# Turning the last eight row blocks of LN(x) with transposing DMAs instead of TensorE

## The chip, the cores and the metric

The kernel runs on one core of a Trainium2 chip. The time is that of the whole launch on the device in microseconds (us); a lower one is better. A core has five engines that each work through a queue of their own in order: TensorE (PE, matmuls), VectorE (DVE), ScalarE (ACT), GpSimd (POOL) and SyncE (SP), which here issues nearly all DMAs. They wait for each other by semaphores.

## The reference

The block computes, for 2048 tokens of width 512:

```python
h  = x + A(layernorm(x))            # A: 32 heads of 16, full softmax, then wo
h2 = h + B(layernorm(h))            # B: a gated MLP (gMLP) with a 2048x2048 mixing over tokens
# A:
qkv = (LN(x) @ wqkv)                # x: [2048, 512], wqkv: [512, 1536]
p = softmax(q @ k.T * 16**-0.5);  o = p @ v;  out = o @ wo
# B:
z = gelu(LN(h) @ w_in);  z1, z2 = halves of z
g = w_sp @ layernorm(z2) + b_sp;  out = (z1 * g) @ w_out
```

All inputs and the output are float32. The change concerns the first step alone: `LN(x)` and its way into the products with `wqkv`.

## The kernel before

**Precision.** A float32 matrix is held as two float16 matrices, a high part (the value rounded) and a low part (what the rounding left). A product is three matmuls (`mm3`, L107 to L109): high by high, high by low, low by high.

**The prologue** makes `LN(x)`, turns it so that the features lie on the partitions (`xT`, high part `xT[0]`, low part `xT[1]`), and multiplies it with `wqkv`. The 2048 rows are 16 blocks of 128 (block `sb`). For one block:

- `load_x` fetches it (tile `xg`), `stats` (L385, DVE) takes its mean and variance, `scales` computes the reciprocal root for four blocks at once (about a dozen tiny DVE instructions, L114 to L131, and `nb`, L401).
- `normal` (L412, ACT) normalizes the block in place.
- `turn_x` is `turn_only` (four 128x128 float32 transposes on PE, L424, into the PSUM tile `tp`) and `put_x`: ACT copies `tp` to the high part (L433), and DVE subtracts that from `tp` into the low part (L431).

A projection is 12 matmuls over 512 columns into one PSUM bank `acc`, of which there are three in turn. `proj_v(sb)` makes the rows of v of one block; `take_v` (DVE, L492) copies them out and SP stores them (L493, `v_scr`). `proj_qk(b, n, i)` makes k (i = 1) or q (i = 0) of a quarter n (blocks 4n to 4n+3) for the weight column block b; its take is a high part on ACT (L458), a low part on DVE (L461), and a store on SP (L464). For k with n < 2, `sums` makes two more ACT copies (`kf`, L472 and L473), later a sum on GpSimd (L476 to L479). The take of a projection is written into the middle of the next one.

**The weights** of the q and k columns come by column block b: `load_wqk(b)` (SP, L345, two DMAs of 256 KB), `weigh_wqk(b)` (two DVE reductions, L352, then two GpSimd products `each`, L356), `measure(b)` (a PE matmul, L374, then small DVE instructions), and `put_wqk(b)`, which scales and splits them. Block 0 is used in the loop below; block 1 is loaded in its last round.

**Order.** Every engine's order is the order of the code (`manual_schedule`); nothing is sorted later. The loop around the change runs over `g` = 0, 1, 2 with a = 4g and b = 4g+4, so that round g multiplies blocks a to a+3 and prepares blocks b to b+3. Below, v8 is `proj_v(8)`, and k2 and q2 are the products of quarter 2. PE's order in the rounds is: round 1: v4 to v7, k1, q1; round 2: v8 to v11, k2, q2; then v12, `measure(1)`, v13, k3, q3, v14, v15. After that come 24 projections for b = 1 to 3, among which the first row maxima of the attention are taken, and the attention itself from about 160 us.

In each round 1 and 2 the blocks b, b+1 are normalized before k and q, and turned inside q; blocks b+2, b+3 are normalized after q and turned inside the first v projection of the next round (or of the code after the loop).

Of the kernel before, what the change touches and what calls it, by code (L numbers as in the profile page):

```python
# [11 lines left out]
F16 = mybir.dt.float16  # L12
I32 = mybir.dt.int32
AF = mybir.ActivationFunctionType
# [5 lines left out]
P = 128  # L20
S = 2048
D = 512
# [8 lines left out]
DB = D // P  # L31
# [28 lines left out]
def block_kernel(ctx: ExitStack, tc: tile.TileContext, x, wqkv, wo, w_in, w_sp4, b_sp, w_out, out):  # L60
# [7 lines left out]
    nc = tc.nc  # L68
# [118 lines left out]
    def load_q(g):  # L187
        hg, qb = divmod(g, NQ)
        c = slice(qb * 512, (qb + 1) * 512)
        qst[g] = qpool.tile([RG + KM, 2, 512], F16, name="qst")  # L190
        for j in range(3):
            for t in range(2):
                h0 = DH * head(hg, 0, t)
                nc.sync.dma_start(
                    qst[g][RG * t + j:RG * t + KS:3, :, :],
                    q_scr[(0, 1, 0)[j], h0:h0 + 2 * DH, c].rearrange("(p r) s -> r p s", r=DH))
# [72 lines left out]
    with ExitStack() as pre:  # L269
        p2 = pre.enter_context(tc.tile_pool(name="pre_2", bufs=2))  # L270
        pc = pre.enter_context(tc.tile_pool(name="pre_c", bufs=1))
# [2 lines left out]
        pt = pre.enter_context(tc.tile_pool(name="pre_pt", bufs=2, space=PSUM))  # L274
        more[3] = more[4] = lambda: pt.tile([P, 512], F32, name="tp")

        xT = [pc.tile([P, DB, S], F16, name=f"xT{i}") for i in range(2)]
        wv = [pc.tile([P, DB, D], F16, name=f"wv{i}") for i in range(2)]
        w4 = wqkv.rearrange("(a p) c -> p a c", p=P)
        xs, xns, wqk, wvs = {}, {}, {}, {}  # L280
# [3 lines left out]
        def load_x(sb):  # L284
            xs[sb] = p2.tile([P, D], F32, name="xg", tag="row", bufs=10)
            nc.sync.dma_start(xs[sb], x[sb * P:(sb + 1) * P, :])
# [53 lines left out]
        def load_wqk(b):  # L340
            raws[b] = []
            for i in range(2):
                t = p2.tile([P, 512], F32, name="wg", tag="row", bufs=10)
                t = t.rearrange("p (a c) -> p a c", a=DB)
                nc.sync.dma_start(t, w4[:, :, i * D + b * P:i * D + (b + 1) * P])  # L345
                raws[b].append(t)

        def weigh_wqk(b):

            most = p2.tile([P, 2], F32, name="most")  # L350
            for i in (1, 0):
                nc.vector.tensor_reduce(most[:, i:i + 1], raws[b][i], axis=AX.XY, op=ALU.max,  # L352
                                        apply_absolute_value=True)
            each = p2.tile([P, 2, P], F32, name="each")
            for i in range(2):
                nc.gpsimd.tensor_scalar(each[:, i], ident, most[:, i:i + 1], 1.0,  # L356
                                        op0=ALU.mult, op1=ALU.mult)
            measures.append(lambda: measure(b, each))

        def put_wqk(b):  # L360

            wqk[b] = [p2.tile([P, 2, DB, P], F16, name=f"wqk{i}") for i in range(2)]
            for i in (1, 0):
                hi, lo, t, by = wqk[b][0][:, i], wqk[b][1][:, i], raws[b][i], sizes[b][:, i:i + 1]
                if b:
                    nc.gpsimd.tensor_scalar(t, t, by, 1.0, op0=ALU.mult, op1=ALU.mult)
                    split(hi, lo, t, "pool", "pool")
                else:
                    scaled(hi, lo, t, by, None if i else "pool")
# [11 lines left out]
        def stats(mv, *blocks):  # L381

            for sb in blocks:
                st = p2.tile([P, 6], F32, name="st")
                nc.vector.bn_stats(st, xs[sb])  # L385
                nc.vector.bn_aggr(mv[0][:, len(mv) - 1, :], st)
                mv.append(sb)

        def moments(n):
            return [p2.tile([P, n, 2], F32, name=f"mv{n}")]  # L390

        def scales(mv, between=lambda: None):

            t, *blocks = mv
            n = len(blocks)
            rs = rstd_of(p2, t[:, :, 1], n, between, up=HN_UP)
            nb = p2.tile([P, n], F32, name=f"nb{n}")
            if n == 1:
                nc.vector.tensor_scalar(nb, rs, t[:, 0, 0:1], -1.0, op0=ALU.mult, op1=ALU.mult)
            else:  # L400
                nc.vector.scalar_tensor_tensor(nb, t[:, :, 0], -1.0, rs, op0=ALU.mult, op1=ALU.mult)  # L401

            def normal(*which, on="act"):

                for sb in which:
                    j = blocks.index(sb)
                    xns[sb] = xs.pop(sb)
                    if on == "dve":
                        nc.vector.tensor_scalar(xns[sb], xns[sb], t[:, j, 0:1], rs[:, j:j + 1],
                                                op0=ALU.subtract, op1=ALU.mult)  # L410
                        continue
                    nc.scalar.activation(xns[sb], xns[sb], AF.Identity,  # L412
                                         bias=nb[:, j:j + 1], scale=rs[:, j:j + 1])

            return normal
# [3 lines left out]
        def turn_only(sb):  # L419

            xn = xns.pop(sb)
            tps[sb] = tp = pt.tile([P, 512], F32, name="tp").rearrange("p (d s) -> p d s", d=DB)
            for d in range(DB):
                nc.tensor.transpose(tp[:, d, :], xn[:, d * P:(d + 1) * P], ident)  # L424

        def put_x(sb, *which):

            c = slice(sb * P, (sb + 1) * P)
            for i in which:
                if i:  # L430
                    nc.vector.tensor_sub(xT[1][:, :, c], tps[sb], xT[0][:, :, c])  # L431
                else:
                    nc.scalar.activation(xT[0][:, :, c], tps[sb], AF.Copy)  # L433

        def turn_x(*blocks):

            for sb in blocks:
                turn_only(sb)
                put_x(sb, 0, 1)
# [108 lines left out]
        def proj(kind, *which, then=lambda: None, at=1, **kw):  # L548

            def between(d):  # L550
                if d == 0 and rest:
                    rest.pop(0)()
                if d == 1:
                    if takes:
                        takes.pop(0)()
                if d == at:
                    then()

            takes.append(kind(*which, between, **kw))
# [11 lines left out]
        normal = scales(mv[0])  # L571
        normal(0, on="dve")
        measure_wv()
        turn_only(0)
        stay_warm(3)
        put_x(0, 0)
        normal(1, on="dve")
        put_wv(0, "act")
# [4 lines left out]
        stay_warm(2)  # L583
        put_wv(1, "act")
        put_x(0, 1)
        put_x(1, 0)
        normal(2, 3)
# [24 lines left out]
        for g in range(3):  # L612
            a, b = 4 * g, 4 * g + 4
            mv = moments(4)
            if g:
                proj(proj_v, a)
                turn_x(a + 2, a + 3)
                if g == 1:
                    load_x(14)
                    load_x(15)  # L620
                stats(mv, b, b + 1)
                proj(proj_v, a + 1)
                stats(mv, b + 2, b + 3)
                proj(proj_v, a + 2)
                normal = scales(mv)
                normal(b, b + 1)
                proj(proj_v, a + 3)
            else:
                proj(proj_v, 2, on_act=True)
                stats(mv, 4, 5, 6)  # L630
                measures.pop(0)()
                stats(mv, 7)
                put_wqk(0)
                proj(proj_v, 3, on_act=True)
            if g == 1:
                load_q(0)
            proj(proj_qk, 0, g, 1)
            if not g:
                normal = scales(mv)
                normal(b, on="dve")  # L640
                normal(b + 1)
            if g == 2:
                load_wqk(1)
            proj(proj_qk, 0, g, 0, then=lambda: turn_x(b, b + 1), at=1 if g else 2)
            if not g:
                load_x(12)
                load_x(13)
            normal(b + 2, b + 3)
        weigh_wqk(1)
        proj(proj_v, 12)  # L650
        turn_x(14, 15)
        load_wqk(2)
        load_wqk(3)
        measures.pop(0)()
# [12 lines left out]
        for j in range(24):  # L667
            b, n, i = 1 + j // 8, j // 2 % 4, 1 - j % 2
# [119 lines left out]
    with ExitStack() as at:  # L788
# [256 lines left out]
        for n in range(0, len(units), 2):  # L1045
# [53 lines left out]
            for tok in PAIR if len(later) < 2 else ():  # L1099
                i = int(tok[-1]) if tok[-1].isdigit() else 0  # L1100
# [16 lines left out]
                elif tok == "H":  # L1117
                    a = 0 if first else 256
# [47 lines left out]
    with ExitStack() as mid:  # L1166
# [73 lines left out]
        with tc.manual_schedule(engines={E.PE, E.Activation, E.DVE, E.Pool, E.SP}):  # L1240
# [3 lines left out]
            for k in range(NB):  # L1244
                sb, new = row[k], row.get(k + 2)
# [358 lines left out]
```

## Time and profile before

| | |
|---|---|
| runs | 1713.07, 1714.01, 1714.47 us; median 1714.01 |
| profiled execution, first to last instruction (span) | 1712.3 us |
| PE busy | 1699.5 us, 99% |
| DVE / ACT / POOL busy | 85% / 77% / 48% |
| granted TensorE clock | full throughout |

The span is the time from the first to the last instruction of the one execution that was profiled, and the trace gives no other time for it; the median of the runs is 1.7 us above it. Times in rows count from the span's start. A row of the timeline reads: start, length, engine, line and operation, output<-inputs, sizes, how many instructions are merged in it (x2), and in brackets how long the engine stood idle before it and what released it. SPq is SP's issue of DMAs; its length is that of the issuing, not of the transfer.

### The profile page before, as it was taken

What the parts mean: (1) busy time and instruction counts of PE and PEld (TensorE: products, weight loads), DVE (VectorE), ACT (ScalarE), POOL (GpSimd) and SP (SyncE); (2) the same over time, 40 slices, a digit from 0 to 9 for tenths busy, and PEclk for the clock granted to TensorE, in tenths of its full rate; (3) what the DMA queues carried; (4) which work ended last, traced back from release to release, by engine and by line L of the source; (5) the groups of instructions that cost most, each with busy time, mean ns of one, the idle gap of its engine ahead of it and who ended that gap; (6) DMA issues with size and microseconds to landing.
All of it is one profiled execution on the core that took longest, in us unless ns stands there. A gap on an engine that the chain in (4) does not pass through costs nothing.

```text
span 1712.3 us, 36689 instructions
## 1 busy us (share of the span) xinstructions
PE 1699.5 (99%) x13508; PEld 644.7 (38%) x13508; DVE 1452.5 (85%) x3051; ACT 1317.5 (77%) x2584; POOL 813.6 (48%) x1062
## 2 busy tenths in 40 slices
PE   9999999999999999999999999999999999999999
PEld 4533222222222222222222222222225666656665
DVE  7688999999999999999999999999936787543444
ACT  4334999999999999999999999999995545211111
POOL 1231867776673267687767776400002766300100
PEclk9999999999999999999999999999999999999999
DMA  5534332342221244344434444300114454664551
GB/s 185 167 94 144 103 89 68 101 94 82 81 68 25 56 118 117 104 144 125 130 113 124 132 140 130 80 13 19 37 39 124 140 173 140 233 234 156 198 217 44
DMA packets 189309, 196.03 MB, mean 114 GB/s; under 512 B 67496, under 2 KB 140008, under 8 KB 189128
## 3 DMA queue, kind: packets, MB, share of 16 engines
q1 hardware_dynamic: 186824, 188.04, 36.8%
q10 hardware_dynamic: 2304, 5.64, 0.8%
q8 instruction: 106, 1.74, 0.4%
q14 instruction: 75, 0.61, 0.1%
HBM read 122.10 MB, written 65.93 MB: 110 GB/s over the span
## 4 chain that ended last, share of the span: by engine, by line
PE 78%; DVE 12%; DMA 3%; POOL 2%; ACT 2%; SPq 2%; issue 1%; ACTq 0%; POOLq 0%; DVEq 0%
PE pv L830 26%; PE s L805 17%; PE m L223 9%; DVE mx L228 7%; PE acc L107 4%; PE g L108 4%; PE g L109 4%; PE g L107 4%; PE acc L109 4%; PE acc L108 4%; DMA rc<-r_scr 1%; DVE ab L237 1%; DVE og L840 1%; SPq L723 1%; DVE rs_t L124 1%
## 5 line engine op out<-in xcount | busy, mean ns | idle before, releaser
L814 ACT ACTIVATE pt<-s 128x512 f32<-128x512 f32 x1968 | 1006.2, 637 | 5.5 <-PE m L223 4.3
L228 DVE TENSOR_REDUCE mx<-m 128x1 f32<-128x512 f32 x1510 | 947.5, 682 | 11.7 <-PE m L223 2.9
L805 PE MATMUL s<-qst,kst 50*128 50x512 f16 x2048 | 604.2, 379 | 0.2
L830 PE MATMUL pv<-pt,vst 128*32 128x256 f32 (+1 forms) x6056 | 598.1, 466 | 4.1 <-DVE og L840 1.3
L223 PE MATMUL m<-kst,qst 48*128 48x512 f16 x1510 | 452.4, 381 | 0.0
L805 PEld LDWEIGHTS <-kst 50*128 50x128 f16 x2048 | 132.0, 94 | 352.1 <-issue 323.7
L830 PEld LDWEIGHTS pv<-pt,vst 128*32 128x32 f32 x6056 | 119.5, 108 | 290.7 <-issue 277.3
L223 PEld LDWEIGHTS <-qst 48*128 48x128 f16 x2048 | 159.2, 93 | 173.6 <-issue 124.2
L223 PE MATMUL m<-uvs,qst 48*128 48x512 f16 x504 | 190.5, 380 | 0.6 <-DVE mx L228 0.6
L245 POOL TENSOR_SCALAR nm<-nm 128x16 f32<-128x16 f32 x32 | 6.6, 206 | 358.8 <-DVE nm L242 358.8
L237 DVE CUSTOM_DVE_ANT_0 ab<-m,ab 128x512 f32<-128x512 f32 x252 | 170.5, 677 | 2.7 <-ACT ab L233 2.7
L233 ACT ACTIVATE ab<-m 128x512 f32<-128x512 f32 x252 | 157.3, 624 | 15.5 <-PE m L223 14.8
L1368 ACT ACTIVATE pr<-pr,up 128x304 f32<-128x304 f32 (+1 forms) x32 | 17.0, 574 | 109.2 <-DVE up L1322 109.2
L991 POOL TENSOR_TENSOR op<-raw,op 128x512 f16<-128x512 f32 x80 | 92.9, 1161 | 6.0
L914 POOL TENSOR_TENSOR raw<-raw 128x512 f32<-128x512 f32 (+1 forms) x84 | 83.3, 991 | 6.7
L919 POOL TENSOR_TENSOR acc_sp<-acc_sp,raw 128x512 f32<-128x512 f32 x63 | 80.4, 1277 | 4.5
L109 PE MATMUL acc<-wi,hT 128*128 128x344 f16 x256 | 79.1, 309 | 0.3 <-DVE hT L104 0.3
L107 PE MATMUL acc<-wi,hT 128*128 128x344 f16 x256 | 79.1, 309 | 0.0
L108 PE MATMUL acc<-wi,hT 128*128 128x344 f16 x256 | 79.1, 309 | 0.0
L1510 POOL TENSOR_TENSOR pr<-pr,z 128x344 f32<-128x344 f32 x8 | 7.3, 914 | 145.9 <-DMA whole<-squares 108.3
L911 POOL TENSOR_SCALAR raw<-raw 128x512 f32<-128x512 f32 (+1 forms) x88 | 52.3, 594 | 19.7 <-DMA raw<-in_wqkv 12.4
L1509 DVE TENSOR_TENSOR pr<-g,v 128x344 f32<-128x344 f32 x8 | 4.1, 517 | 66.6 <-PE g L109 63.5
(247 smaller groups left out, 2292.9 us busy)
## 6 DMA issues: line engine op xcount, KB each, us to landing
raw<-in_w_sp SPq DMA_DIRECT2D x128, 256.0 KB
s_scr<-op SPq DMA_DIRECT2D x64, 256.0 KB
op<-s_scr SPq DMA_DIRECT2D x32, 512.0 KB
a_scr<-op SPq DMA_DIRECT2D x48, 256.0 KB
op<-a_scr SPq DMA_DIRECT2D x24, 512.0 KB
o_scr<-og SPq DMA_DIRECT2D x64, 128.0 KB
qst<-q_scr SPq DMA_DIRECT2D x192, 32.0 KB
kst<-k_scr SPq DMA_DIRECT2D x48, 128.0 KB
```

What stands on the lines that cost most here:

```text
L107: nc.tensor.matmul(ps, lh, rh, start=first, stop=False, **kw)
L108: nc.tensor.matmul(ps, lh, rl, start=False, stop=False, **kw)
L109: nc.tensor.matmul(ps, ll, rh, start=False, stop=last, **kw)
L223: nc.tensor.matmul(acc, q[r, p, c], keys[r, p], start=True, stop=True)
L228: nc.vector.reduce_max(at(t, e if t else e - 1), acc, axis=AX.X)
L233: nc.scalar.activation(ab[0], acc, AF.Abs)
L237: nc.vector.tensor_tensor_reduce(ab[0], acc, ab[0], 0.5, LOW, ALU.add, ALU.max, at(0, 0))
L805: nc.tensor.matmul(s, kst[hg % 2][r, p, kb * P:(kb + 1) * P], qst[hg * NQ + qb][r, p, :], start=True, stop=True)
L814: nc.scalar.activation(pts[p, kb][:, t, :], s, AF.Exp, scale=scales_[hg // 2])
L830: nc.tensor.matmul(pv[0][32 * j:32 * j + 32, a:b], vst[hg % 2][:, c:c + 32], pts[j % 2, kb][:, j // 2, a:b], start=kb == 0, stop=kb == NB - 1,
L914: pool.tensor_mul(got[0] if n else acc, got[0], got[0])
L991: chores.append((lambda: pool.tensor_sub(t[0][:, 1], of(), t[0][:, 0]), TT))
```

## The change

Blocks 8 to 15 are no longer turned by PE. In rounds 1 and 2, right after the scales, all four blocks are normalized, and each is split as it lies: ACT casts it to float16 (the high part), GpSimd subtracts that from it (the low part), both into one SBUF tile `xp` of 128x1024 float16, and SP issues one transposing DMA from `xp` to the place of the block in `xT`, high and low together. `xp` has the pool's two buffers, so the third block's cast waits until the first block's DMA has landed. Blocks 6 and 7 and those before them are turned by PE as before.

```diff
-        xT = [pc.tile([P, DB, S], F16, name=f"xT{i}") for i in range(2)]
+        xTs = pc.tile([P, 2, DB, S], F16, name="xT")
+        xT = [xTs[:, i] for i in range(2)]
...
+        def split_x(*blocks):
+
+            for sb in blocks:
+                xn = xns.pop(sb)
+                xp = p2.tile([P, 2, D], F16, name="xp")
+                nc.scalar.activation(xp[:, 0], xn, AF.Copy)
+                nc.gpsimd.tensor_sub(xp[:, 1], xn, xp[:, 0])
+                nc.sync.dma_start_transpose(
+                    xTs[:, :, :, sb * P:(sb + 1) * P].rearrange("p i d s -> p (i d) s"),
+                    xp.rearrange("p i c -> p (i c)"))
...
             if g:
                 proj(proj_v, a)
-                turn_x(a + 2, a + 3)
+                if g == 1:
+                    turn_x(a + 2, a + 3)
...
                 proj(proj_v, a + 2)
                 normal = scales(mv)
-                normal(b, b + 1)
+                for sb in range(b, b + 4):
+                    normal(sb)
+                    split_x(sb)
                 proj(proj_v, a + 3)
...
             if g == 2:
                 load_wqk(1)
-            proj(proj_qk, 0, g, 0, then=lambda: turn_x(b, b + 1), at=1 if g else 2)
-            if not g:
+            if g:
+                proj(proj_qk, 0, g, 0)
+            else:
+                proj(proj_qk, 0, g, 0, then=lambda: turn_x(b, b + 1), at=2)
                 load_x(12)
                 load_x(13)
-            normal(b + 2, b + 3)
+                normal(b + 2, b + 3)
         weigh_wqk(1)
         proj(proj_v, 12)
-        turn_x(14, 15)
         load_wqk(2)
```

On SP, the queue that issues the DMAs, in round 2 before: the four stores of v8 to v11 (L493), then the two loads of the weight block 1 (L345), then the stores of k2 and q2, then the loads of weight blocks 2 and 3.

```order
L493 DMA v_scr<-v 128x512 x4
L345 DMA wg<-in_wqkv 128x4x128 x2
L464 DMA k_scr<-part 128x2x512
L464 DMA q_scr<-part 128x2x512
L345 DMA wg<-in_wqkv 128x4x128 x4
```

The same place now; the line numbers are 1 to 16 higher in the changed kernel, L505 being the store of v and L346 the load of weights:

```order
L505 DMA v_scr<-v 128x512 x2
L443 DMA_TRANSPOSE xT<-xp 128x8x128 x4
L505 DMA v_scr<-v 128x512 x2
L346 DMA wg<-in_wqkv 128x4x128 x2
L476 DMA k_scr<-part 128x2x512
L476 DMA q_scr<-part 128x2x512
L346 DMA wg<-in_wqkv 128x4x128 x4
```

The four transposes of blocks 12 to 15 stand ahead of the last two stores of v and of the loads of weight block 1.

On ACT, round 1 before: normalize 8 and 9 (L412), take k1 (L458), copy blocks 8 and 9 out of PSUM (L433), normalize 10 and 11, the two `kf` copies (L472, L473), take q1, copy blocks 10 and 11.

```order
L412 ACTIVATE xg<-xg,nb_613,rs_r_601 128x512 x2
L458 ACTIVATE part<-acc 128x512
L433 ACTIVATE xT_175<-tp 128x4x128 x2
L412 ACTIVATE xg<-xg,nb_613,rs_r_601 128x512 x2
L472 ACTIVATE kf_694<-acc 64x512
L473 ACTIVATE kf_694<-acc 64x512
L458 ACTIVATE part<-acc 128x512
L433 ACTIVATE xT_175<-tp 128x4x128 x2
```

The same place now, with the normalizations in L413 and the new casts in L441:

```order
L413 ACTIVATE xg<-xg,nb_612,rs_r_600 128x512
L441 ACTIVATE xp<-xg 128x512
L413 ACTIVATE xg<-xg,nb_612,rs_r_600 128x512
L441 ACTIVATE xp<-xg 128x512
L413 ACTIVATE xg<-xg,nb_612,rs_r_600 128x512
L441 ACTIVATE xp<-xg 128x512
L413 ACTIVATE xg<-xg,nb_612,rs_r_600 128x512
L441 ACTIVATE xp<-xg 128x512
L470 ACTIVATE part<-acc 128x512
L484 ACTIVATE kf_695<-acc 64x512
L485 ACTIVATE kf_695<-acc 64x512
L470 ACTIVATE part<-acc 128x512
```

The takes of k1 and q1 (L470) now stand behind all four casts, the third and fourth of which wait for the DMAs of the first and second block.

## The prediction

> **What bounds the kernel now.** I read the page's totals first, then the chain of work that ended last over the first 200 us, then PE's waits there, then the timeline of the other engines.
>
> ```profile
> span 1712.3 us, 36689 instructions
> PE 1699.5 (99%) x13508; PEld 644.7 (38%) x13508; DVE 1452.5 (85%) x3051; ACT 1317.5 (77%) x2584; POOL 813.6 (48%) x1062
> PEclk9999999999999999999999999999999999999999
> ```
>
> PE is the bound overall. What a change in the prologue is worth must be read there, in the chain (start, length, what):
>
> ```profile
> 46.21 0.87 PE tp L424 x8
> 50.97 0.87 PE tp L424 x8
> 63.50 0.87 PE tp L424 x8
> 68.26 0.87 PE tp L424 x8
> 69.13 0.43 PE m L374 x2
> ```
>
> These four transposes of two blocks each are on the chain that sets the end, and they are what the change takes away from PE: 4 x 0.87 = 3.48 us. The only wait of PE between 55 and 170 us is this one, at the very end of the stretch (engine, line, waited for: total, times, longest):
>
> ```profile
> PE pv L1114 <- DVE part L461: 0.8, 1, 0.8
> ```
>
> So from 55 to 160 us PE has no slack in which a later start could disappear. Whatever makes PE late in the prologue makes the end late by as much.
>
> Next, what PE will wait for once its own work there is shorter. The tightest neighbour is `measure(1)`, the matmul between v12 and v13:
>
> ```profile
> 55.64 6.16 SPq L493 DMA_DIRECT2D v_scr<-v  x4
> 62.30 0.96 SPq L345 DMA_DIRECT2D wg<-in_wqkv  x2
> 66.17 1.28 DVE L352 TENSOR_REDUCE most<-wg 128x1 f32<-128x512 f32 x2 [0.28 <-DMA wg<-in_wqkv]
> 67.55 0.72 POOL L356 TENSOR_SCALAR each<-ident,most 128x128 f32<-128x128 f32 x2 [14.04 <-DVE most L352]
> 68.97 0.60 PE L374 MATMUL m<-each,every 128*128 128x256 f32 x2
> ```
>
> Read downwards this is a chain of its own: SP issues the loads of weight block 1 until 63.26, DVE is released by their landing at 66.17 (2.91 us later), GpSimd ends `each` at 68.27, and PE arrives at 68.97. The whole reserve is 0.70 us. That already caps the gain: a PE that is 3.48 us earlier arrives at 65.49 and stands until 68.27, so the change brings 0.70 us at most unless this chain gets earlier too.
>
> **The change part by part.** The rows for the durations:
>
> ```profile
> 23.63 1.33 ACT L316 ACTIVATE wqk<-wg,size 128x512 f16<-128x512 f32 x2 [3.61 <-DVE size L302]
> 42.92 1.52 ACT L412 ACTIVATE xg<-xg,nb,rs_r 128x512 f32<-128x512 f32 x2 [7.68 <-issue]
> 45.01 0.60 ACT L458 ACTIVATE part<-acc 128x512 f16<-128x512 f32 x1 [0.56 <-ACT xg L412]
> 49.07 0.58 ACT L472 ACTIVATE kf<-acc 64x512 f32<-64x512 f32 x1
> 49.66 0.59 ACT L473 ACTIVATE kf<-acc 64x512 f32<-64x512 f32 x1
> 50.27 0.60 ACT L458 ACTIVATE part<-acc 128x512 f16<-128x512 f32 x1
> 60.15 1.52 ACT L412 ACTIVATE xg<-xg,nb,rs_r 128x512 f32<-128x512 f32 x2 [7.62 <-DVE nb L401]
> 52.35 1.16 POOL L479 TENSOR_TENSOR part<-uv,part 128x512 f16<-128x512 f32 x1
> 50.91 0.69 DVE L461 SCALAR_TENSOR_TENSOR part<-acc,part 128x512 f16<-128x512 f32 x1 [2.30 <-ACT part L458]
> 53.28 0.68 DVE L385 BATCH_NORM_STATS2 st<-xg 128x6 f32<-128x512 f32 x1
> 63.72 0.37 SPq L464 DMA_DIRECT2D k_scr<-part  x1
> 83.42 1.00 SPq L493 DMA_DIRECT2D v_scr<-v  x2
> 94.39 2.45 SPq L181 DMA_DIRECT2D raw<-v_scr  x2
> ```
>
> *Removed:* the PE transposes (3.48 us, on the path), and their copies on ACT and subtractions on DVE, which PE does not wait for today. *Added:* eight casts on ACT at 0.67 us (half of the 1.33 us row), eight subtractions on GpSimd at 1.16 us (9.3 us in all, on an engine that stood idle 14.04 us before `each`), and eight transposing DMAs of 256 KB on SP. Busy time is not the matter; the order is. Let T be the time from the issue of one transpose to its landing, and I the time for which SP is busy issuing it.
>
> *Round 1.* Block 8: normalization from 42.92 (0.76), cast (0.67), subtraction (1.16): its DMA is issued at 45.51. With two buffers, ACT cannot cast block 10 before 45.51 + T. Behind that wait in ACT's queue stand the rest of the four (0.67 + 0.76 + 0.67), the take of k1 (0.60), two `kf` copies (1.20 by their starts) and the take of q1 (0.60); then DVE's low part of q1 (0.69): ended at 50.7 + T. On DVE the statistics of blocks 12 to 15 stand behind it. Before, they started at 53.28 and ACT's normalization of block 12 at 60.15, 6.87 us later. Now block 12 is normalized from 57.57 + T.
>
> *Round 2.* 0.76 + 0.67 + 1.16: block 12's DMA is issued at 60.16 + T. Again ACT waits T for a buffer, then casts block 14, normalizes 15, casts it, and GpSimd subtracts (0.67 + 0.76 + 0.67 + 1.16 = 3.26): block 15's DMA is issued at 63.42 + 2T. Only behind it, in SP's queue, come two stores of v (1.00), the two loads of weight block 1 (0.96), and 2.91 us until they land: 68.29 + 2T + I, against 66.17 before. DVE's reductions, GpSimd's `each` and `measure(1)` follow as before, and the reserve of 0.70 us goes off: **PE comes to `measure(1)` later by 2.12 - 0.70 + 2T + I = 1.42 + 2T + I.** What PE saved, and its shorter waits for blocks 8 to 12, all vanish in that one wait. Behind it stand v13, k3 and everything else; on DVE, behind the reductions, the low part of q2; on SP, the loads of blocks 2 and 3.
>
> *T and I.* No row shows a transposing DMA. The rows of the chain that show landing times:
>
> ```profile
> 743.34 1.94 DMA sums<-o_scr
> 866.40 2.46 DMA s_scr<-op
> 1322.88 7.05 DMA o<-o_scr
> ...
> s_scr<-op SPq DMA_DIRECT2D x64, 256.0 KB
> wg<-in_wqkv SPq DMA_DIRECT2D x12, 256.0 KB
> ```
>
> 1.94 us is the shortest, 2.46 us belongs to a plain 256 KB out of SBUF, 7.05 us is the longest. The weight loads above are of the same size, in 512-byte pieces, in the same stretch: the second is issued from 62.78 and has landed at 66.17, 3.39 us. A transpose cuts its rows into pieces too, so I take T = 3.4, with ends 1.94 and 7.05. For I the ends are half of the 1.00 us row or less (0.37 in the shortest store) and half of the 2.45 us row, 1.22, where a tile is cut into 128-byte pieces; I take 1.22. So 1.42 + 6.8 + 1.22 = 9.4 us.
>
> *The clock.* v12 can start when block 12 has landed, 60.16 + 2T = 67.0, and ends 2.6 us later (from the starts of k1 and q1 below); PE then stands idle from 69.6 to about 78.4. What an idle PE costs beyond its idling has one row, the first 30 matmuls of the kernel:
>
> ```profile
> 1.20 8.18 PE L526 MATMUL acc<-idle 128*128 128x512 bf16 x30 [1.20 <-DVE idle L520]
> 42.16 0.38 PE L107 MATMUL acc<-xT,wqk 128*128 128x512 f16 x1
> 44.76 0.38 PE L107 MATMUL acc<-xT,wqk 128*128 128x512 f16 x1
> ```
>
> Twelve matmuls take 2.60 us between the last two rows, 0.217 each; 30 would take 6.7 us and took 8.18. A PE that had stood idle lost 1.5 us. Ends 0 and 1.5; I take 1.5, since the gap here is of 9 us. [...]
>
> **Sum.** 9.4 + 1.5 = 11 us slower. On the profiled execution's 1712.3 us that is 1723.3; the runs' median of 1714.0 lies 1.7 us above the span, so 1725.0.
>
> **Rivals.** 0.2% of this time, about what a measurement here can tell from no change, is 3.4 us.
>
> 1. *The loads are not held up, and PE just saves its transposes.* Place: SP's queue. If the second weight load were issued by 62.8 as now, PE would wait for `each` until 68.27: 0.7 us gained, 1713.3. If DVE's and GpSimd's part came 2.8 us earlier as well, the whole 3.5 us would be kept: 1710.5. Against it: even with T = I = 0 the sum gives +1.42, since block 15 cannot be split before 63.4. For it: DVE loses eight subtractions, which could bring the statistics forward, though they wait for q1's take. It decides at a weight landing of 66.9.
> 2. *The transposes are slow.* T at or above the longest landing row, 7.05: 1.42 + 14.1 + 1.22 + 1.5 = 18.2, 1732 or more. For it: eight squares of 128x128 have to be turned in one DMA, in pieces smaller than in any row. Against it: 16 DMA engines share them. [...]
> 3. *The delay is given back later*, in the attention, where DVE and ACT are nearly full as well. Then about 1714. Against it: DVE, ACT and GpSimd all hang on the same `measure(1)` and q2, and get no head start.
>
> **How the numbers follow.** The forecast (weights held up, T between 1.94 and 7.05: 1719.7 without the clock's term and with I = 0.37, to 1732.2 with both) has 0.75. Rival 2 has 0.13. Rival 1 with 0.7 us and rival 3, both within 0.2%, have 0.08 together; rival 1 in full, faster by just over 0.2%, has 0.04. So slower 0.88, same 0.08, faster 0.04. The range 1718 to 1734 holds the forecast's own ends and the near part of rival 2.
>
> **What would show it.** In the changed trace: DMA_TRANSPOSE rows on SP with their landing seen as PE's, ACT's or SP's releaser; ACT idle before the third cast of each round; the two weight loads issued near 71 us instead of 62.3; DVE's reductions of weight block 1 near 75; and one PE wait of 8 to 9 us for `each` on GpSimd before `measure(1)`, after which all rows stand about 11 us later than before, with a few matmuls at a slower step. The prediction is wrong if T is far from 3.4 us (each us of it counts twice), or if the weight loads are issued before 66 us.

## The result and the profile after

| | before | changed |
|---|---|---|
| median of 5 runs | 1713.07 us (1712.55 to 1714.47) | 1725.86 us (1725.47 to 1727.06) |
| span of the profiled execution | 1712.3 us | 1725.3 us |
| time, changed to before | | 1.0075, 95% interval 1.0063 to 1.0086 |

The change makes the kernel 0.75% slower. The forecast was 1725.0 us, the range 1718 to 1734. It started from 1714.0, the median of the first three runs before; with five runs that median is 1713.07. The profiled execution is the slowest of the five runs (1727.06 us), so its rows are compared with its own span: 13.0 us more than before.

The totals of the changed kernel, in the same lines as before:

```profile
span 1725.3 us, 36633 instructions
PE 1699.8 (99%) x13476; PEld 642.5 (37%) x13476; DVE 1447.3 (84%) x3043; ACT 1318.2 (76%) x2584; POOL 820.8 (48%) x1070
PEclk9899999999999999999999999999999999999999
```

PE runs 32 instructions less (13508 to 13476) and is busy as long as before, 1699.8 against 1699.5 us. The digit 8 in the second slice of the clock row (43 to 86 us) is new: a part of that slice ran at a lower clock.

PE's waits between 40 and 165 us (waited for: total, times, longest). Before, there was one, of 0.8 us:

```profile
PE m L375 <- POOL each L357: 9.4, 1, 9.4
PE acc L107 <- DMA xT<-xp: 2.6, 2, 1.5
PE acc L107 <- ACT kf L485: 1.8, 1, 1.8
```

Most of it is the wait before `measure(1)`. The timeline of the engines that it waited for, in the changed kernel:

```profile
45.73 7.98 SPq L443 DMA_TRANSPOSE xT<-xp  x4
49.16 0.63 ACT L441 ACTIVATE xp<-xg 128x512 f16<-128x512 f32 x1 [2.62 <-DMA xT<-xp]
64.57 7.90 SPq L443 DMA_TRANSPOSE xT<-xp  x4
67.91 0.63 ACT L441 ACTIVATE xp<-xg 128x512 f16<-128x512 f32 x1 [2.49 <-DMA xT<-xp]
72.56 1.01 SPq L505 DMA_DIRECT2D v_scr<-v  x2
73.66 1.03 SPq L346 DMA_DIRECT2D wg<-in_wqkv  x2
77.83 1.28 DVE L353 TENSOR_REDUCE most<-wg 128x1 f32<-128x512 f32 x2 [6.61 <-DMA wg<-in_wqkv]
79.21 0.72 POOL L357 TENSOR_SCALAR each<-ident,most 128x128 f32<-128x128 f32 x2 [8.02 <-DVE most L353]
79.98 1.22 PE L375 MATMUL m<-each,every 128*128 128x256 f32 x2 [9.36 <-POOL each L357]
```

Read downwards, it is the chain of the prediction. In each round the first DMA is issued (45.73, 64.57), ACT stands until it has landed before it casts the third block (49.16, 67.91: T = 3.43 and 3.34 us), and SP gives out the four DMAs over 8 us. In round 2 the weight loads stand behind them, are issued at 73.66 instead of 62.30, and `measure(1)` runs at 79.98 instead of 68.97: 11.0 us late.

The granted clock (the column of 0.79, 0.50 and 0.97, behind the engines' busy times) in three stretches of the changed kernel:

```profile
75.00:75.50 0.50, 0.00 (x0) 0.00 (x0) 0.00 (x0) 0.00 (x0) 0.00 (x0) 0.79 0.87 138
80.00:85.00 5.00, 5.00 (x12) 2.14 (x13) 1.71 (x6) 0.00 (x0) 2.48 (x4) 0.50 0.81 235
85.50:86.00 0.50, 0.50 (x3) 0.20 (x2) 0.00 (x0) 0.00 (x0) 0.44 (x2) 0.97 1.07 399
```

While PE stands, its clock falls to half (within the first stretch), and it stays there for 5.5 us after PE is busy again: twelve matmuls in 5 us where a full clock does 23 (shown with the experiments). At the first matmul of k3 the delay has grown from 11.0 to 13.8 us (71.99 to 85.83).

What becomes of it later is read from two groups of PE, the products with v in the attention and those with `wo` behind it, before (L830, L747) and after (L846, L763). The last times in a row are the starts of the first and the last instruction:

```profile
L830 PE MATMUL pv<-pt,vst x6056: 379/403/618, 164.8 to 1293.1; 128*32 128x256 f32 x126, 128*32 128x512 f32 x70
L747 PE MATMUL acc<-wo,o x168: 376/379/390, 1294.4 to 1428.9; 128*128 128x512 f16 x168
```

```profile
L846 PE MATMUL pv<-pt,vst x6056: 378/403/618, 178.6 to 1306.9; 128*32 128x256 f32 x126, 128*32 128x512 f32 x70
L763 PE MATMUL acc<-wo,o x168: 376/379/390, 1308.9 to 1441.9; 128*128 128x512 f16 x168
```

The attention starts 13.8 us late and its last product with v 13.8 us late: 1128 us give nothing back. The products with `wo` start 14.5 us late, the last of them 13.0 us late, and 13.0 is the difference of the spans.

### The profile page after: what moved, and what is told of

Its sections match the earlier page's. It is cut to its first block, busy times and chain, and to the rows that moved or that the text cites. A ratio compares the mean times of both kernels' runs of the same rounds, so it can differ in the third digit from the quotient of the medians.

```text
span 1725.3 us, 36633 instructions
## 1 busy us (share of the span) xinstructions
PE 1699.8 (99%) x13476; PEld 642.5 (37%) x13476; DVE 1447.3 (84%) x3043; ACT 1318.2 (76%) x2584; POOL 820.8 (48%) x1070
## 4 chain that ended last, share of the span: by engine, by line
PE 74%; DVE 14%; POOL 4%; issue 3%; DMA 2%; ACT 2%; SPq 1%; ACTq 0%; POOLq 0%; DVEq 0%
PE pv L846 25%; PE s L821 17%; PE m L223 9%; DVE mx L228 7%; PE g L108 4%; PE g L109 4%; PE g L107 4%; PE acc L107 3%; PE acc L108 3%; PE acc L109 3%; DVE ab L237 1%; DVE og L856 1%; DVE rs_t L124 1%; PE acc L763 1%; DMA raw<-in_w_sp 1%
## 5 line engine op out<-in xcount | busy, mean ns | idle before, releaser
L830 ACT ACTIVATE pt<-s 128x512 f32<-128x512 f32 x1968 | 1007.1, 638 | 5.4 <-PE m L223 4.3
L846 PE MATMUL pv<-pt,vst 128*32 128x256 f32 (+1 forms) x6056 | 598.1, 466 | 4.1 <-DVE og L856 1.3
L846 PEld LDWEIGHTS pv<-pt,vst 128*32 128x32 f32 x6056 | 119.5, 108 | 290.1 <-issue 276.8
L912 POOL TENSOR_SCALAR raw<-raw,figs 128x512 f32<-128x512 f32 (+1 forms) x84 | 55.5, 664 | 9.0 <-DMA raw<-in_wo 7.9
```

The source lines that it names most:

```text
L830: nc.scalar.activation(pts[p, kb][:, t, :], s, AF.Exp, scale=scales_[hg // 2])
L846: nc.tensor.matmul(pv[0][32 * j:32 * j + 32, a:b], vst[hg % 2][:, c:c + 32], pts[j % 2, kb][:, j // 2, a:b], start=kb == 0, stop=kb == NB - 1,
```

## The experiments

The theory: the change saves 3.5 us of PE, and loses them and 13 us more because the DMAs of the third and fourth block wait for a buffer and hold up SP, with the loads of weight block 1 behind them; the idle PE then loses clock. The rivals: the other order of normalizations costs the time, or the transposing DMAs themselves do, or their contention. Differences below are those of the medians, against the kernel before, run alongside. Where an expectation names a run by its number, e1 is "the loads ahead", e3 is "both" and e6 is "earlier loads".

### The order alone

All four blocks are normalized together, as in the change, but turned by PE as before.

```diff
-                for sb in range(b, b + 4):
-                    normal(sb)
-                    split_x(sb)
+                normal(b, b + 1, b + 2, b + 3)
...
+            proj(proj_qk, 0, g, 0, then=lambda: turn_x(b, b + 1), at=1 if g else 2)
...
+        turn_x(14, 15)
```

> The kernel before with one part of the change: the four blocks of rounds 1 and 2 are normalized together right after the scales, but they are still turned by PE where PE turned them before, and there is no xp, no GpSimd subtraction and no transposing DMA. Theory (all of the loss is in the DMAs' landing time, seen through the buffers and SP's queue): the two normalizations that move forward, 1.5 us on ACT, fall into ACT's idle time ahead of the take of k; PE never waits, 1712.5 to 1713.7, as before. Rival (normalizing all four together delays ACT's takes and PE's banks by itself): over 1715.

Measured: 1712.87 us against 1713.35, ratio 1.0 (0.9991 to 1.0009). PE's only wait from 40 to 165 us is the one of before:

```profile
PE pv L1126 <- DVE part L473: 0.8, 1, 0.8
```

So the four normalizations in one go cost nothing that can be measured. The 12.8 us are in the splitting and the DMAs.

### The loads ahead of the transposes

```diff
                 proj(proj_v, a + 2)
+                if g == 2:
+                    load_wqk(1)
                 normal = scales(mv)
...
-            if g == 2:
-                load_wqk(1)
```

> The changed kernel, with one thing moved: in round 2 the two loads of weight block 1 are issued before the scales, so on SP they stand ahead of the four transposing DMAs. Theory (SP's queue held the loads back, and through DVE and GpSimd the matmul measure(1)): DVE's reductions of weight block 1 no longer wait for a DMA; what ends last before measure(1) is then the take of k2, which stands behind the fourth cast on ACT (cast ends 69.9 in the changed kernel): low part of k2 71.2, reductions 72.4, products 73.2, so PE waits about 2.7 us there instead of 9.4 and keeps its clock. k3 starts near 76.2 instead of 85.8: about 9.6 us less than the changed kernel, 1716 to 1717 us. Rival 1 (the late takes on ACT and the buffers are what costs, not the loads): PE's wait stays over 6 us and the time over 1722. Rival 2 (the transposes crowd the DMA engines, so the loads would be slow wherever they stand): the reductions still wait for the DMA, later than 70 us, time over 1720.

Measured: 1719.81 us against 1713.11, ratio 1.0041 (1.0027 to 1.0055): 6.7 us slower, where 3 to 4 were expected. Two of PE's waits are:

```profile
PE acc L107 <- DMA xT<-xp: 3.9, 2, 2.4
PE m L375 <- POOL each L357: 2.7, 1, 2.7
```

The timeline of SP and PE in round 2:

```profile
62.95 1.87 SPq L346 DMA_DIRECT2D wg<-in_wqkv  x2
64.91 8.87 SPq L443 DMA_TRANSPOSE xT<-xp  x4
69.18 0.39 PE L107 MATMUL acc<-wv,xT 128*128 128x512 f16 x1 [2.39 <-DMA xT<-xp]
```

The wait for `each` is 2.7 us, as forecast: the loads no longer stand behind the transposes, but DVE and GpSimd reach `each` only behind ACT's late take. What was not forecast: the transpose of block 12, issued right behind the two loads, lands 4.27 us after its issue (64.91 to 69.18) instead of 3.4, and the clock (0.88 and 0.71 in these stretches) drops here too:

```profile
75.00:75.50 0.50, 0.50 (x4) 0.23 (x3) 0.17 (x1) 0.00 (x0) 0.00 (x0) 0.88 1.10 358
78.50:79.00 0.50, 0.50 (x4) 0.16 (x2) 0.00 (x0) 0.00 (x0) 0.50 (x1) 0.71 1.18 194
```

### Four buffers instead of two

```diff
-                xp = p2.tile([P, 2, D], F16, name="xp")
+                xp = p2.tile([P, 2, D], F16, name="xp", bufs=4)
```

> The changed kernel with four buffers for xp instead of two; the loads of weight block 1 stay behind the transposes on SP. Theory (the buffer wait counts T = 3.4 us in each of two rounds, the place of the loads the rest): ACT no longer waits for a landing; block 12 is normalized near 59.3 instead of 61.8, block 15's DMA is issued near 66.2 instead of 71.2, the loads land near 72.4, measure(1) comes near 74.5. PE still waits 6 to 7 us there and its clock still drops, 2.8 us. 1713.1 + 5.5 + 2.8 less the 0.8 us that is given back later: about 1720.5; 1718 if the clock does not drop. Rival (only the place of the loads matters, the buffers do not): 1725 to 1726, as the changed kernel.

Measured: 1721.00 us against 1713.11, ratio 1.0046 (1.0032 to 1.0059), within half a us of the expectation. The wait in question is now:

```profile
PE m L375 <- POOL each L357: 6.9, 1, 6.9
```

The clock falls in the first of these stretches (0.83) and comes back in the second (0.68):

```profile
72.00:73.50 1.50, 0.00 (x0) 0.00 (x0) 1.00 (x2) 0.00 (x0) 0.00 (x0) 0.83 0.35 121
79.50:80.00 0.50, 0.50 (x3) 0.25 (x2) 0.00 (x0) 0.00 (x0) 0.50 (x2) 0.68 1.02 309
```

ACT no longer stands for a landing, and 4.9 us of the loss are gone. The wait that remains is SP's: four DMAs at over 1.2 us each (median 1.27), ahead of the loads.

### Both

The two edits above together.

> Both edits: the loads of weight block 1 ahead of the transposes, and four buffers for xp. Theory: every wait named in the prediction is gone but those for the first block of each group, which lands 3.4 us after its issue: PE waits 1.7 us for block 8 and 0.7 for block 12, and about 0.3 before measure(1). Of the 3.5 us of PE transposes that were saved 0.6 remain: 1712 to 1713, no difference to the kernel before that can be measured. Rival (waits that these two edits do not touch, on ACT or in the transfers, hold PE): 1716 or more. Rival (the first blocks' waits do not count): 1710.

Measured: 1712.19 us against 1713.11, ratio 0.9995 (0.9986 to 1.0004). PE's wait for `each` is gone, and the clock stays full (1.00 from 60 to 100 us). What remains is waiting for the DMAs, once in each round:

```profile
PE acc L107 <- DMA xT<-xp: 3.2, 2, 1.7
```

In round 2 the first transpose is issued at 61.96, behind the loads, and PE reads its block at 66.31, 4.35 us later.

This names the cause. With both reasons taken away the whole loss is gone, though the eight casts, subtractions and DMAs are still there; with one of them taken away, 6.7 and 7.9 us remain. The gain of 3.48 us is not had either: PE waits 3.2 us for the first block of each round.

### Keeping PE busy in the gap

Forty matmuls on a constant tile, ahead of `measure(1)`; they write a bank that nobody reads.

```diff
+        hot = bank(2)
+        for _ in range(40):
+            nc.tensor.matmul(hot, idle[:, :P], idle, start=True, stop=True)
         measures.pop(0)()
```

> The changed kernel, with 40 matmuls on the tile idle (128x512, about 8.6 us at full clock) put into PE's queue between v12 and measure(1), where PE stands 9.4 us; their result is not used. Theory (the 9.4 us of idling halves PE's granted clock for about 5 us after it, which costs the 2.8 us by which the delay grows between measure(1) and k3): the clock stays full, v13 takes 2.6 us instead of 4.8, and the time falls by 2.5 to 2.8 us to about 1723. Rival (the slow matmuls come from something else, such as the operands' arrival or the DMA traffic at that time): v13 stays slow and the time at 1725 to 1726.

Measured: 1723.33 us against 1713.11, ratio 1.0064 (1.005 to 1.0077). PE's rows in the timeline:

```profile
70.39 8.80 PE L672 MATMUL m<-idle 128*128 128x512 bf16 x40
79.94 0.70 PE L375 MATMUL m<-each,every 128*128 128x256 f32 x2 [0.75 <-POOL each L357]
```

The stretch in which the clock was 0.50 in the changed kernel, here at 1.00:

```profile
80.00:85.00 5.00, 5.00 (x23) 2.39 (x24) 2.46 (x7) 0.00 (x0) 3.05 (x4) 1.00 0.80 228
```

`measure(1)` starts at the same time, and behind it 23 matmuls run in 5 us instead of 12. The loss shrinks from 12.8 to 10.2 us: the clock's part is about 2.6 us.

### Earlier loads, and a faster first block

Two further edits were meant to shorten the remaining waits of "both". First the loads of weight block 1 a round earlier, so that the stores and transposes of round 2 have SP to themselves:

```diff
             if g == 1:
                 load_q(0)
+                load_wqk(1)
```

> Four buffers for xp as in e3, and the loads of weight block 1 already in round 1, after the loads of q, so that they have landed long before the transposes of round 2. In e1 and e3 block 12 landed 4.3 us after its issue, with the two weight loads just ahead of it in the queue, against 3.4 us where nothing was ahead. Theory (the loads' transfer, not their issue, delayed that transpose): T of block 12 is 3.4 us again, PE's wait for block 12 falls from 1.66 to about 0.75 us, and the time by 0.9 us to 1711.3. Rival (the 4.3 us come from something else in round 2): wait and time as in e3, 1712.2.

Measured: 1713.45 us against 1713.35, ratio 1.0001 (0.9992 to 1.001); a miss. In round 2 the rows of SP and PE are:

```profile
60.89 1.71 SPq L505 DMA_DIRECT2D v_scr<-v  x2
62.70 5.47 SPq L443 DMA_TRANSPOSE xT<-xp  x4
66.59 0.39 PE L107 MATMUL acc<-wv,xT 128*128 128x512 f16 x1 [1.68 <-DMA xT<-xp]
```

The loads went away, and two stores of v took their place: DVE had waited 1.59 us for an earlier store of v, issued at 57.14 just behind the loads, before it could make them. SP is free at 62.6 only, and the block lands 3.89 us after its issue.

Second, on top of that, the first block of each round in fewer steps: ACT writes the high part straight from x, DVE normalizes and subtracts.

```diff
+                        nc.vector.tensor_scalar(xf, x0, t[:, j, 0:1], rs[:, j:j + 1],
+                                                op0=ALU.subtract, op1=ALU.mult)
+                        nc.scalar.activation(xp[:, 0], x0, AF.Identity,
+                                             bias=nb[:, j:j + 1], scale=rs[:, j:j + 1])
+                        nc.vector.tensor_sub(xp[:, 1], xf, xp[:, 0])
```

> As e6, and the first block of each group is made ready faster: ACT writes its high part straight from x (normalizing and casting in one), DVE at the same time normalizes it in float32 and then subtracts; GpSimd is left out for that block. Its DMA is issued near 44.4 instead of 45.5 in round 1, and 1.1 us earlier in round 2 too. Theory (the lead of the first block's DMA is what is left): PE waits 0.4 to 0.5 us for block 8 instead of 1.58 and not at all, or under 0.2 us, for block 12; up to 0.3 us is lost for the takes of v that DVE does later. Of the 3.5 us 2.5 to 3 us remain: 1709.5 to 1710.5, faster than the kernel before by 0.15 to 0.2%. Rival (DVE's later takes of v hold PE's banks by as much): 1711 to 1712.

Measured: 1713.64 us against 1713.35, ratio 1.0002 (0.9993 to 1.0011); a miss again. The first DMA and its reader in the timeline:

```profile
44.67 1.37 SPq L449 DMA_TRANSPOSE xT<-xp  x1
49.54 0.39 PE L107 MATMUL acc<-wv,xT 128*128 128x512 f16 x1 [1.43 <-DMA xT<-xp]
```

Two stretches between them (the last two columns are the DMA engines' share and GB/s):

```profile
47.00:47.50 0.50, 0.50 (x4) 0.20 (x2) 0.00 (x0) 0.47 (x2) 0.50 (x1) 1.00 4.17 67
47.50:48.00 0.50, 0.50 (x3) 0.10 (x1) 0.00 (x0) 0.50 (x2) 0.39 (x1) 1.00 0.00 0
```

The DMA is issued 1.1 us earlier, and the block lands 4.87 us after its issue, at 49.54 instead of 49.20 in the run before. In between, packets hold the DMA engines (4.17) at only 67 GB/s, and then nothing moves for half a microsecond: a transfer stalled. Why is open; no run here tells it. In round 2 the DMA does not even start earlier (62.94 against 62.70): the two stores of v hold SP until 62.84, and PE waits 1.42 us.

### Half the size

Each block turned by two DMAs of 128x512, the high and the low part apart, on top of "both".

```diff
-                nc.sync.dma_start_transpose(
-                    xTs[:, :, :, sb * P:(sb + 1) * P].rearrange("p i d s -> p (i d) s"),
-                    xp.rearrange("p i c -> p (i c)"))
+                for i in range(2):
+                    nc.sync.dma_start_transpose(xTs[:, i, :, sb * P:(sb + 1) * P], xp[:, i])
```

> As e3, but the high and the low part of a block are turned by a DMA each, 128x512, instead of one of 128x1024: sixteen DMAs of half the size. Asks what T is made of. If it is mostly fixed (landing), the low part lands 3.0 to 3.4 us after its issue and PE's wait for block 8 falls only a little, by 0.2 us or so; if it goes by what is to be turned, the low part lands in 1.7 to 2 us and the wait for block 8 goes from 1.58 to about 0.1. SP's issue should be 0.6 to 0.7 us each if it goes by the squares, 1.26 if fixed. Time 1710.5 to 1712.5.

Measured: 1721.26 us against 1713.35, ratio 1.0047 (1.0033 to 1.0061): 7.9 us slower where a gain was expected. The DMA's own row (ns: shortest, median, longest):

```profile
L444 SPq DMA_TRANSPOSE xT<-xp x16: 1199/1220/2129, 44.0 to 75.4; - x16
```

Two of PE's waits:

```profile
PE acc L107 <- DMA xT<-xp: 4.3, 2, 4.0
PE acc L107 <- DVE v L503: 1.7, 1, 1.7
```

A row of SP's timeline, round 2:

```profile
66.13 10.50 SPq L444 DMA_TRANSPOSE xT<-xp  x8
```

Issuing a transpose of half the size takes 1.22 us, nearly the 1.26 of a whole one. Eight in a round keep SP for twice as long (11.3 us in round 1, against 5.5 in "both"). The stores of v behind them come late, DVE waits for a buffer of v (1.97 us at 57.73), and PE for DVE. The transposes of round 2 stand behind those late stores and the loads: the first is issued at 66.13 instead of 61.96, and PE waits 4.0 us for it. The clock drops too, at 70.28, and is back at 73.69 (means of 0.78 from 70.00 to 70.50 and 0.81 from 73.50 to 74.00). This is the mechanism of the changed kernel with other transfers as the victims.

### Two blocks by PE, two by DMA

The runs so far say what these transposing DMAs need: a reader that comes later than their landing (3.3 to 4.9 us after the issue), a buffer for each, and no urgent transfer behind them (1.2 to 1.3 us of SP for each). The third and fourth block of each round have that: they are read only in the next round. The first two are turned by PE as before; the last two are split by DVE (cast) and GpSimd, issued behind the loads. This is "the order alone" with:

```diff
-                turn_x(a + 2, a + 3)
+                if g == 1:
+                    turn_x(a + 2, a + 3)
...
-                nc.scalar.activation(xp[:, 0], xn, AF.Copy)
+                nc.vector.tensor_copy(xp[:, 0], xn)
...
             if g == 2:
                 load_wqk(1)
+            if g:
+                split_x(b + 2, b + 3)
             proj(proj_qk, 0, g, 0, then=lambda: turn_x(b, b + 1), at=1 if g else 2)
...
-        turn_x(14, 15)
```

> All four blocks of a group are normalized together as in the change, but in rounds 1 and 2 the first two are turned by PE inside q, as before, and only the last two are split (high part cast on VectorE, low part on GpSimd) and turned by a DMA, behind the loads of weight block 1. PE does half of what the change saves: 2 x 0.87 = 1.74 us. Theory (a DMA lands 3.4 us after its issue starts, and costs nothing where its reader comes later than that): the DMA of block 10 is issued at about 47 us and read at 52.5, that of block 15 at about 65 and read at 70, so PE waits for no xT, the matmul of measure(1) waits under 0.5 us, and the clock stays full: 1711.0 to 1712.0, that is 1.3 to 2 us less than before. Rival (another use of the engines beside PE makes up for what PE saves): 1713 or more, with waits of PE in the stretch from 45 to 75 us.

Measured: 1711.05 us (11 runs, 1710.58 to 1711.78) against 1713.24 (15 runs, 1712.67 to 1714.15), ratio 0.9986 (0.9977 to 0.9995). It beats both kernels; against the one before by 2.2 us, or 0.14% by the ratio. The engines' totals:

```profile
PE 1697.7 (99%) x13492; PEld 643.6 (38%) x13492; DVE 1453.2 (85%) x3051; ACT 1315.5 (77%) x2580; POOL 817.6 (48%) x1066
```

PE's only wait from 40 to 165 us:

```profile
PE pv L1128 <- DVE part L473: 0.8, 1, 0.8
```

SP's four transposes and `measure(1)` in the timeline:

```profile
50.07 2.78 SPq L443 DMA_TRANSPOSE xT<-xp  x2
61.83 2.78 SPq L443 DMA_TRANSPOSE xT<-xp  x2
67.93 0.59 PE L375 MATMUL m<-each,every 128*128 128x256 f32 x2
```

The gain agrees with the 1.74 us of transposes that PE is spared; the interval reaches from 0.9 to 3.9 us. PE is busy 1.8 us less than before, waits for nothing new, and comes to `measure(1)` 1.0 us earlier. Since this execution began k1 0.7 us later (42.87 against 42.16), it gained 1.75 us from there to `measure(1)`. The expectation had the DMA of block 10 at 47 us; it is issued at 50.07, behind other transfers, and nobody needs it sooner.

## Why the prediction was right, and where its sizes were off

**The mechanism held.** The weights were held up, all that PE had saved vanished in the wait for `each` (forecast 8 to 9 us, measured 9.4), and everything up to the end of the attention moved by that delay and the clock's. The runs "four buffers", "loads ahead" and "both" show the two reasons of the prediction, ACT's wait for a buffer and SP's queue, each to be worth several us, and the order alone to be worth none.

**T and I.** Forecast 3.4 and 1.22 us; measured 3.43 and 3.34, and 1.26 (the row of the transposes: ns, shortest, median, longest):

```profile
L443 SPq DMA_TRANSPOSE xT<-xp x8: 1232/1257/1372, 45.7 to 71.2; - x8
```

The value taken for T was right by luck: it came from a weight load of the same size, with pieces as the common reason. The pieces are there (from 45 to 50 us two transposes moved 0.52 MB in 2112 packets, all under 512 bytes), but no run shows that T comes from them. The first transpose was issued from 45.73; up to 47.00 us no byte moved, and in the stretch that ends at 48.50 the traffic falls off, between that transfer and the next (last column: GB/s):

```profile
46.75:47.00 0.25, 0.25 (x3) 0.11 (x2) 0.00 (x0) 0.00 (x0) 0.25 (x1) 1.00 0.00 0
48.25:48.50 0.25, 0.00 (x0) 0.00 (x0) 0.00 (x0) 0.00 (x0) 0.00 (x0) 1.00 0.60 115
```

So T is 1.3 us of issuing, 1.4 us of transfer and 0.7 us until the reader is released. For I too the row taken, of a DMA in 128-byte pieces, gave the right number; that pieces make the issue long is not shown, since half the size took 1.22 us as well. Rival 2 falls with T: it needed 7.05 us or more, and eight squares of 128x128 in one DMA landed in 3.4. The transposes were slower than the plain DMAs around them all the same: with the DMA engines full (shares of 1.13 and 1.02), the first transposes moved about 210 GB/s (first row), the weight loads and stores of v about 340 (second row), and the issue of a transpose took 1.26 us against about 0.5 for one of the two stores or loads in the rows above (1.01 and 1.03 us for two):

```profile
47.50:47.75 0.25, 0.08 (x1) 0.00 (x0) 0.00 (x0) 0.00 (x0) 0.00 (x0) 1.00 1.13 210
74.00:74.50 0.50, 0.00 (x0) 0.00 (x0) 0.00 (x0) 0.00 (x0) 0.00 (x0) 1.00 1.02 344
```

**The sum 1.42 + 2T + I.** Forecast 9.4, measured 11.0 us. The step that was short most is round 1's: ACT's queue behind the wait for a buffer. Two rows of ACT in the changed kernel:

```profile
52.44 0.59 ACT L484 ACTIVATE kf<-acc 64x512 f32<-64x512 f32 x1 [0.76 <-DVE part L473]
61.78 0.81 ACT L413 ACTIVATE xg<-xg,nb,rs_r 128x512 f32<-128x512 f32 x1 [7.53 <-DVE nb L402]
```

The working let the two `kf` copies follow the take of k1 at once. They also wait for DVE's low part of k1, which itself waits for that take: 0.76 us. Block 12 is normalized at 61.78 instead of the forecast's 60.97. The rest of the 1.6 us lies in round 2: from the normalization of block 12 to the issue of its DMA it took 0.2 us longer, and the loads, issued at 73.66, landed 0.23 us later behind their issue (77.83 - 74.69 = 3.14, forecast 2.91); gaps of 0.1 us on SP and the longer I make up what is left.

**The clock.** Forecast 1.5, measured 2.8 us by the growth of the delay from `measure(1)` to k3, 2.6 us by the dummy matmuls. The step that failed is its model, the 30 first matmuls: they show what a cold start cost once, not how long the clock stays low. (The slow ones are at the start: seven in the 2.81 us that PE was busy before 4.00, 0.40 us each. The clock column says 1.00 there all the same, so "full throughout", as said of the kernel before, leaves this start out.) The clock's edges are worked out from the mean clock of the stretches: a mean of 0.79 over 0.5 us is 0.29 us at full and 0.21 at half speed. They lie at 75.29 and 85.53 us in the changed kernel, 75.38 and 78.79 with the loads ahead, 72.99 and 79.82 with four buffers, 70.28 and 73.69 with half the size. The distances are 10.24, 3.41, 6.83 and 3.41 us: whole multiples of 3.41. So in these four runs the clock stayed low for three, one, two and one times 3.41 us. That time did not begin with the wait: the clock fell 4.7, 3.4, 5.3 and 4.3 us after PE had begun to wait. Nor did it end a fixed time after the wait: the clock came back 5.5, 4.2, 5.2 and 3.7 us after PE was busy again. What sets the two moments no run here tells.

**Rival 3** (given back later) is the smallest part: of 13.8 us, 0.8 came back, all of it behind the attention. Another 0.7 us was lost before the first product with `wo`, and 1.5 came back up to the last one. There PE comes back to `wo` every 10.0 us; in the kernel before, four of the steps took 10.4 to 10.5 us, in the changed kernel one took 10.3. What lengthens them was not tested. With this the account closes: 11.0 + 2.8 - 0.8 = 13.0 us. The forecast's 11 was 1.6 short in the chain, 1.3 short in the clock, and 0.8 over here, 2 us in all. That the forecast time lies only 0.9 us below the measured median is in part luck: by the medians of five runs the change costs 12.8 us, 1.8 more than forecast, and the 1714.0 from which the forecast started was 0.9 too high.

**Rival 1** (the loads are not held up) was priced at 0.7 or 3.5 us of gain. "Both" makes its condition true, with no wait for `each` left, and its median is 0.9 us less, not to be told from no change. What its price left out is the landing of the first block: 3.2 us of waits for `xT`, nearly all that PE saves.

## What to carry to other kernels

Before work is moved from a full engine to a DMA, look in the DMA queue for what will stand behind it, and in the buffers for who waits until it has landed: here four transposes that held the queue for 7.9 us ahead of two loads (5 us of issuing, the rest waiting for a buffer), and the waits around them, turned 3.5 us saved into 12.8 us lost. The price of a transposing DMA is its issue (1.2 to 1.3 us each here) and its landing (3.3 to 4.9 us for a whole block here), against the moment at which the result is read; where the reader comes late enough, as in the last version, PE waits for none of it. A long idle gap on PE can cost more than its length: after the one of 9.4 us the clock stayed at half for another 5.5 us.

## What the runs showed of the hardware that was not expected

- SP's issue of a transposing DMA out of SBUF took 1.26 us for 128x1024 float16 and 1.22 us for 128x512 (medians; the longest were 1.37 us in the changed kernel and 2.13 with half the size): at these two sizes a price per DMA and hardly one per byte.
- The landing of the same transpose took 3.4 us with nothing just ahead of it on the queue, 3.9 us behind two stores and 4.3 us behind two loads. That the transfers ahead are the reason was not tested by itself.
- In one run the clock halved with no wait of PE longer than 2.66 us: in "loads ahead" PE waited 2.39 us until 69.18 and 2.66 until 74.60, and the clock fell at 75.38. In "both", where PE's waits before 100 us were 1.58 and 1.66 us, it stayed at 1.00.
- Once (the first DMA of the faster first block) a transfer stalled for over a microsecond (at most 10 GB/s from 47.25 to 48.75 us); its cause is open.
